# First expert: units in a meander, one sum of y over two FF tiles; relu(1 - e) by ScalarE in the second expert's regular groups; a new order

## The chip, the cores and the metric

One core of one Trainium2 chip runs the whole program. The metric is the device time of one execution in microseconds: the median of three runs of the kernel before is 793.62 us (793.28 to 793.9). TensorE is written PE, VectorE DVE, ScalarE ACT, GpSimd POOL, SyncE SP.

## The reference

Attention with hashed buckets, then two dense experts on the same 1536 tokens:

```
q_bucket, k_bucket = 6 sign bits of q @ proj, k @ proj          # 2 x 8 heads, 768 x 64
attn   = softmax(where(q_bucket == k_bucket, q @ k.T / 8, -1e9)) @ v
x      = attn, heads side by side                               # 1536 x 512
xn     = x / sqrt(mean(x * x) + 1e-6) * rms_g
g, val = xn @ w_gate, xn @ w_val                                # FF 1536
y      = (g * sigmoid(g) * val) @ w_out                         # the first expert
h      = y @ w_in                                               # FF 2048
out    = where(h > 0, h, exp(min(h, 0)) - 1) @ w2_out           # the second expert
```

The weights arrive as 64-bit floats and are turned into 32-bit words on the chip. Every product of both experts is made of three matmuls on pairs of fp32r tiles, a rounded part ("hi") and what the rounding left ("lo"): hi x hi, hi x lo, lo x hi.

## The kernel before, in words

**Attention** goes over 8 pairs of heads, 6 units of two query tiles each: scores (`ps_s`), their maximum by DVE, exp by ACT, transposes (`ps_p`), hi and lo parts by ACT and DVE or POOL, and the product with v (`ps_v`).

**The first expert** has 12 FF tiles of 128. Three of them form a regular group (`hidden`, group 0). The other nine are units of their own, n = 0 to 8: `pair(q, j, prio)` takes both batches at once for half of the columns, j = 0 or 1, and makes two 2 x 2 products out of seven (banks `ps_wA`, `ps_wC`, `ps_wE`, 6 matmuls of 384 columns for each product, L1520). It leaves two activated tiles h, o = 0 for column block j and o = 1 for block 2 + j, in the pool `ptp` of `PTS` = 4 tiles. `reduce1` then multiplies such a tile with w_out for each of the m = 0 to 3 output slices (L1160, bank `ps_y`) and DVE adds the bank to the running sum `ya` in SBUF (L1172). After the last unit `hi` and `lo` of `reduce1` split `ya` into the tiles `y` (L1177 by ACT, L1181 by DVE), which the second expert reads. The order of the units before is n = 0 to 8, and j = 0, 1 within each n; every unit's tiles are summed alone:

```
n, first, last = (groups[0][2], True, False) if g == 0 else (1, False, g == ("w", (0, NPW[0] - 1)))
```

**The second expert** has two regular groups of two FF tiles, each over four column blocks of 384 (`hidden`, L1067), and then six units of `pair`. In a regular group ACT makes e = exp(h) (L1095), `d2` on DVE makes min(e, 1) - 1 (L1104), `d3` adds max(h, 0) (L1110), then ACT and DVE split the result (L1116, L1120), and `reduce2` multiplies with w2_out (L1220). Beside the first of these groups `spread_t` combines the blocks of `ya` and splits the results for the second expert's units (L1260, L1267, L1271, on POOL, DVE and ACT), and the weights of the regular groups are converted by `c1` to `c5`, `hi` and `lo` of `weights` (L964 to L1016).

**The order of the work** is written out by hand: each piece of work is a task of the class `Plan`, and the table `ORDER` says in which order the tasks are issued. An engine works through its own tasks in that order; a task waits for what it reads and for a free buffer of its pool. The pools around the change: `ps1` (four PSUM banks, for `ps_wA`, `ps_wC`, `ps_wE`, `ps_h`), `ps2` (two double banks, for `ps_y` and `ps_o`), `ptp` (four h tiles), and `hlf` with `H3S` = 14 tiles of 3 KB, for loads and converted weights.

Of the kernel before, what the change touches and what calls it, by code (L numbers as in the profile page):

```python
# [9 lines left out]
F32R = mybir.dt.float32r  # L10
# [10 lines left out]
SLOTS, H3S, PTS = 22, 14, 4  # L21
# [209 lines left out]
]  # L231


# [1588 lines left out]
```

## Time and profile before

| what | us |
|---|---|
| median of 3 runs | 793.62 |
| the profiled execution, whole | 793.52 |
| its span | 791.7 |
| PE busy | 773.1 (98%) |
| DVE busy | 699.9 (88%) |
| ACT busy | 518.1 (65%) |
| POOL busy | 474.6 (60%) |

The span begins with attention (0 to some 230 us), then comes the first expert's regular group (to 300), its nine units (to some 530), the second expert's regular groups, and from 586 on the second expert's units. PE's busy time counts matmuls that overlap their neighbours and have stretched ends, so 98% doesn't mean that PE is at its peak: how many matmuls fit into a stretch tells more. The granted TensorE clock is full nearly throughout (0.999).

### The profile page before, as it was taken

Reading aid. Unit: us, or ns where it says so; the run is one execution under the profiler, and the core shown is the slowest. Engines: PE = TensorE matmul, PEld = TensorE weight load, DVE = VectorE, ACT = ScalarE, POOL = GpSimd, SP = SyncE. Lnnn points to the kernel's source line nnn. Section 1 sums busy time; section 2 is a strip of 40 time slices with the busy share of each in tenths; the row PEclk is TensorE's granted clock in tenths of the full one; section 3 lists DMA queues with packets and bytes.
Section 4 is the critical chain, followed back from the end, with each engine's and each line's share of the span. In section 5 each row is a group of like instructions: output and inputs, shape, how many; then the busy total and the mean of one; then the engine's idle time right before and its main releaser. Section 6 shows DMA issues by size and latency. Waiting matters only on the chain.

```text
span 791.7 us, 13077 instructions
## 1 busy us (share of the span) xinstructions
PE 773.1 (98%) x4618; PEld 726.1 (92%) x4618; DVE 699.9 (88%) x1147; ACT 518.1 (65%) x1078; POOL 474.6 (60%) x480
## 2 busy tenths in 40 slices
PE   8999999999999999999999999978999999999998
PEld 7999899998999999999999999967899889988987
DVE  7898999999985976889989899999888989888885
ACT  7999999989984636554444554556456666657553
POOL 7898899989886277555545554454534453633520
PEclk9999999999999999999999999999999999999999
DMA  5547563461000001222111312311021121131104
GB/s 197 190 134 233 193 176 94 142 180 31 27 28 1 27 1 54 81 81 70 65 52 54 107 55 80 115 45 51 4 80 54 54 81 54 54 97 63 54 2 158
DMA packets 33649, 65.74 MB, mean 83 GB/s; under 512 B 3504, under 2 KB 13104, under 8 KB 33584
## 3 DMA queue, kind: packets, MB, share of 16 engines
q1 hardware_dynamic: 33584, 64.91, 25.9%
q8 instruction: 36, 0.59, 0.3%
q14 instruction: 29, 0.24, 0.1%
HBM read 56.25 MB, written 3.15 MB: 75 GB/s over the span
## 4 chain that ended last, share of the span: by engine, by line
PE 77%; DVE 16%; ACT 3%; issue 2%; DMA 1%; POOL 0%; ACTq 0%; DVEq 0%; POOLq 0%
PE ps_o L1220 16%; PE ps_wA L1520 14%; PE ps_y L1160 10%; PE ps_h L1067 8%; PE ps_wC L1520 7%; PE ps_v L711 6%; PE ps_s L619 6%; PE ps_p L664 5%; PE ps_wE L1520 3%; DVE ya L1172 2%; DVE nm L626 2%; DVE pt L676 2%; DVE y L1181 1%; ACT p L636 1%; DVE h L1598 1%
## 5 line engine op out<-in xcount | busy, mean ns | idle before, releaser
L1458 POOL TENSOR_TENSOR W<-wf,W 128x256 fp32r<-128x256 f32 x105 | 86.9, 841 | 59.7 <-ACT W L1454 56.0
L1220 PE MATMUL ps_o<-whi,h 128*128 128x512 f32 (+1 forms) x388 | 119.6, 389 | 2.4 <-DVE h L1120 2.4
L1160 PE MATMUL ps_y<-h,whi 128*128 128x384 f32 x528 | 115.5, 338 | 4.3 <-DVE ya L1172 4.0
L1520 PE MATMUL ps_wA<-T,W 128*128 128x384 f32 x540 | 108.3, 335 | 0.0
L1160 PEld LDWEIGHTS ps_y<-h,whi 128*128 128x128 f32 x528 | 92.5, 188 | 9.0 <-DVE ya L1172 7.0
L1520 PEld LDWEIGHTS ps_wA<-T,W 128*128 128x128 f32 x540 | 95.3, 188 | 2.1 <-ACT wt L1538 0.3
L626 DVE TENSOR_REDUCE nm<-ps_s 128x1 f32<-128x768 f32 x96 | 91.0, 949 | 4.6 <-PE ps_s L619 3.6
L711 PE MATMUL ps_v<-pt,vv 128*128 128x256 f32 x576 | 94.4, 292 | 0.6 <-DVE pt L676 0.6
L636 ACT ACTIVATE p<-ps_s,nm 128x768 f32<-128x768 f32 x96 | 87.4, 911 | 5.6 <-DVE nm L626 4.1
L619 PE MATMUL ps_s<-tk,tq 128*128 128x384 f32 x384 | 87.2, 349 | 2.2 <-ACT p L636 1.7
L676 DVE TENSOR_TENSOR pt<-ps_p,pt 128x512 fp32r<-128x512 f32 x120 | 80.1, 683 | 8.0 <-ACT pt L672 6.7
L1172 DVE TENSOR_TENSOR ya<-ps_y,ya 128x384 f32<-128x384 f32 x144 | 76.6, 550 | 11.6 <-PE ps_y L1160 11.2
L1220 PEld LDWEIGHTS ps_o<-whi,h 128*128 128x128 f32 x388 | 72.0, 188 | 14.8 <-DVE h L1120 2.8
L664 PE MATMUL ps_p<-ident,p 128*128 128x128 f32 x576 | 82.4, 274 | 1.4 <-DVE pt L676 1.0
L711 PEld LDWEIGHTS ps_v<-pt,vv 128*128 128x128 f32 x576 | 79.6, 189 | 2.7 <-DVE pt L676 1.0
L1377 POOL TENSOR_SCALAR wf<-wf 128x512 f32<-128x512 f32 x51 | 38.1, 748 | 66.5 <-ACT wf L1374 63.5
L1444 POOL TENSOR_TENSOR wf<-wf 128x256 f32<-128x256 f32 x60 | 48.8, 813 | 47.5 <-DVE wf L1393 46.5
L1220 PE MATMUL ps_o<-wlo,h 128*128 128x512 f32 (+1 forms) x194 | 76.1, 392 | 0.0
L672 ACT CAST pt<-ps_p 128x512 fp32r<-128x512 f32 x120 | 68.9, 589 | 8.1 <-PE ps_p L664 5.0
L664 PEld LDWEIGHTS ps_p<-ident,p 128*128 128x128 f32 x576 | 66.6, 141 | 7.1 <-DVE pt L676 1.4
L1233 DVE TENSOR_TENSOR oa<-ps_o,oa 128x512 f32<-128x512 f32 (+1 forms) x85 | 57.1, 680 | 14.9 <-PE ps_o L1220 14.6
L619 PEld LDWEIGHTS ps_s<-tk,tq 128*128 128x128 f32 x384 | 63.1, 189 | 6.2 <-ACT p L636 4.6
(159 smaller groups left out, 1799.0 us busy)
## 6 DMA issues: line engine op xcount, KB each, us to landing
wraw<-in_moe_w_out_dram SPq DMA_DIRECT2D x25, 512.0 KB, 3.3
wraw<-in_moe_w_in_dram SPq DMA_DIRECT2D x16, 512.0 KB, 3.8
qk<-in_heads_dram SPq DMA_DIRECT2D x16, 384.0 KB, 5.1
qq<-in_heads_dram SPq DMA_DIRECT2D x14, 384.0 KB, 5.2
kk<-in_heads_dram SPq DMA_DIRECT2D x14, 384.0 KB, 4.9
wraw<-in_moe_w_gate_dram SPq DMA_DIRECT2D x18, 256.0 KB, 2.8
wraw<-in_moe_w_val_dram SPq DMA_DIRECT2D x18, 256.0 KB, 3.1
tq<-tq SPq DMA_DIRECT2D x21, 192.0 KB, 2.8
```

The lines of the kernel that those rows point to most:

```text
L619: nc.tensor.matmul(st[B_][:, hf, 0:HS], lhsT=tq[:, x, c * 128:(c + 1) * 128], rhs=tk[:, x, hf * HS:(hf + 1) * HS], start=(x == 0), stop=(x ...
L626: nc.vector.tensor_reduce(out=st["nm", u, cc], in_=st[B_][:, :, 0:HS], axis=AX.XY, op=ALU.max, negate=True,)
L636: nc.scalar.activation(out=halves(st["p", u][:, cc]), in_=st.pop(B_)[:, :, 0:HS], func=AF.Exp, bias=st["nm", u, cc], scale=1.0, accum_out= ...
L664: nc.tensor.transpose(out=st[B_][:, o:o + 128], in_=p[:, cc, (2 * n + kt) * 128:(2 * n + kt + 1) * 128], identity=ident,)
L672: nc.scalar.copy(out=st[T_][:, 0], in_=st[B_])
L676: nc.vector.tensor_tensor(out=pt[:, 1], in0=st.pop(B_), in1=f(pt[:, 0]), op=ALU.subtract)
L711: nc.tensor.matmul(st[B_][:, 0:256], lhsT=st["vv", j][:, a, 2 * n + kt, :], rhs=pt[:, x, kt * 256:(kt + 1) * 256], start=(n == seq[0] and ...
L1160: nc.tensor.matmul(s["ps"][:, 0:bw], lhsT=wo[wp][:, ft, m * 128:(m + 1) * 128], rhs=h[:, xp, 0:bw], start=(ft == 0 and i == 0), stop=(ft = ...
L1172: nc.vector.tensor_tensor(out=ya, in0=s["ps"][:, 0:bw], in1=ya, op=ALU.add)
L1220: nc.tensor.matmul(s["ps"], lhsT=h[:, xp, t * 128:(t + 1) * 128], rhs=(wo[wp][ft][:, 0] if reg2(g) else wo[wp][:, ft])[:, ds], start=(ft = ...
L1458: nc.gpsimd.tensor_tensor(out=t[:, 1], in0=blk(*src), in1=f(t[:, 0]), op=ALU.subtract)
L1520: nc.tensor.matmul(s[bk], lhsT=w[:, wp, k], rhs=x[:, xp, cs], start=start and k == 0 and i == 0, stop=k == 1 and i == 2, skip_group_check= ...
```

## The change

Five things change in the code, and the table `ORDER` with them.

1. The units of the first expert run in a meander: (0, j=1), then (0, 0) and (1, 0), then (1, 1) and (2, 1), then (2, 0) and (3, 0), and so on to (7, 1) and (8, 1), and (8, 0) alone. Two units with the same j that follow each other form a row, and `reduce1` takes their two FF tiles into one PSUM bank: six matmuls, and then one addition to `ya`. There are 10 rows, so 80 additions instead of 144; the matmuls stay 432.
2. The last tiles of blocks 1 and 3 come before those of 0 and 2, and the second expert's first group takes the blocks in the order 1, 3, 0, 2.
3. In the second expert's regular groups `a2` on ACT makes relu(1 - e), with a bias from SBUF, in place of `d2` on DVE, and `d3` subtracts it: 16 instructions go from DVE to ACT.
4. The two tiles `bitt` of attention move to the pool `tmp`, under the tag of the units' `wt` tiles, and `H3S` is 15 instead of 14.
5. The gates of the weights' loads follow the new sequence.

```diff
-SLOTS, H3S, PTS = 22, 14, 4
+SLOTS, H3S, PTS = 22, 15, 4
...
-    0, 3, 1, 6, 45, 46, 8, 9, 10, 11, 12, 13, 14, 15, 16, 42, 43, 7, 54, 44, 5, 28, 29, 17, 18, 19, 20, 51, 24, 25,
...
-    bitt = [const.tile([128, S // 2], F32R, name=f"bitt{i}") for i in range(2)]
+    bitt = [tmp.tile([128, S // 2], F32R, tag="wt", name=f"bitt{i}") for i in range(2)]
...
-        def d2():
-            nc.vector.tensor_scalar(
-                out=s["sg"], in0=s["sg"], scalar1=1.0, scalar2=1.0, op0=ALU.min, op1=ALU.subtract
-            )
+        def a2():
+            nc.scalar.activation(out=s["sg"], in_=s["sg"], func=AF.Relu, bias=ones[:, 0:1], scale=-1.0)
...
-                out=s["hf"], in0=s[0][:, 0:bw], scalar=0.0, in1=s["sg"], op0=ALU.max, op1=ALU.add
+                out=s["hf"], in0=s[0][:, 0:bw], scalar=0.0, in1=s["sg"], op0=ALU.max, op1=ALU.subtract
...
-            plan.add("DVE", 0.46, d2, [], [G_], prio)
+            plan.add("ACT", act(bw, 1), a2, [], [G_], prio)
...
-        n, first, last = (groups[0][2], True, False) if g == 0 else (1, False, g == ("w", (0, NPW[0] - 1)))
+        n, first, last = (groups[0][2], True, False) if g == 0 else (len(g), False, (0, NPW[0] - 1) in g)
...
-            wo = st["w", g]["wo"]
+            wo = st["w", g]["wo"] if g == 0 else st["w", ("w", g[ft])]["wo"]
...
+    rows = [[(0, 1)]]
+    for n in range(NPW[0]):
+        rows.append([(x, n % 2) for x in (n, n + 1) if x < NPW[0]])
+    seen = set()
+    for row in rows:
+        for n, j in row:
+            pair((0, n), j, pos)
...
+            pos += 2.0
+            for pg, pb in late:
+                for m in range(KD):
+                    reduce1(pg, pb, m, pos)
+            late = []
+            pos += 1.0
+        late = [(tuple((0, n) for n, _ in row), j), (tuple((0, n) for n, _ in row), 2 + j)]
+    for g in range(1, len(groups)):
...
+        for n, blk in enumerate((1, 3, 0, 2) if g == 1 else (0, 2, 1, 3)):
```

Where the order moves. PE in the middle of the first expert's units, before (`ps_w` are the seven products, `ps_y` the products with w_out; three matmuls are one sum):

```order
L1520 MATMUL ps_wE<-xn,W 128x384 x6
L1160 MATMUL ps_y<-h,whi 128x384 x6
L1520 MATMUL ps_wA<-T,W 128x384 x6
L1160 MATMUL ps_y<-h,whi 128x384 x6
L1520 MATMUL ps_wC<-xn,W 128x384 x6
L1160 MATMUL ps_y<-h,whi 128x384 x6
L1520 MATMUL ps_wA<-xn,W 128x384 x6
L1520 MATMUL ps_wA<-T,W 128x384 x6
L1160 MATMUL ps_y<-h,whi 128x384 x6
```

The same place on PE after the change, where six matmuls are one sum:

```order
L1511 MATMUL ps_wA<-T,W 128x384 x6
L1151 MATMUL ps_y<-h,whi 128x384 x12
L1511 MATMUL ps_wA<-T,W 128x384 x6
L1511 MATMUL ps_wA<-xn,W 128x384 x6
L1151 MATMUL ps_y<-h,whi 128x384 x24
L1511 MATMUL ps_wA<-T,W 128x384 x6
L1511 MATMUL ps_wE<-xn,W 128x384 x6
L1511 MATMUL ps_wC<-T,W 128x384 x6
L1151 MATMUL ps_y<-h,whi 128x384 x12
```

Eight sums of one unit each stood between the products in 24 matmuls; now eight sums of two units each stand there in 48, in fewer and longer runs.

DVE where the first expert meets the second, before (`ya<-ps_y` is a sum, `y_` the split of the finished sum, `sg<-sg` is `d2`, `hf<-ps_h` is `d3`, `h<-hf` a split of an activated tile):

```order
L1172 TENSOR_TENSOR ya<-ps_y,ya 128x384 x2
L1104 TENSOR_SCALAR sg<-sg 128x384
L1172 TENSOR_TENSOR ya<-ps_y,ya 128x384
L1181 TENSOR_TENSOR y_6540<-ya,y_6540 128x384
L1181 TENSOR_TENSOR y_6667<-ya,y_6667 128x384
L1172 TENSOR_TENSOR ya<-ps_y,ya 128x384
L1110 SCALAR_TENSOR_TENSOR hf<-ps_h,sg 128x384
L1172 TENSOR_TENSOR ya<-ps_y,ya 128x384
L1181 TENSOR_TENSOR y_6551<-ya,y_6551 128x384
L1181 TENSOR_TENSOR y_6634<-ya,y_6634 128x384
L1181 TENSOR_TENSOR y_6646<-ya,y_6646 128x384 x2
L1172 TENSOR_TENSOR ya<-ps_y,ya 128x384 x2
```

DVE at that place after the change:

```order
L1172 TENSOR_TENSOR y_6516<-ya,y_6516 128x384
L1172 TENSOR_TENSOR y_6542<-ya,y_6542 128x384
L1172 TENSOR_TENSOR y_6505<-ya,y_6505 128x384
L1172 TENSOR_TENSOR y_6424<-ya,y_6424 128x384
L1172 TENSOR_TENSOR y_6460<-ya,y_6460 128x384
L1163 TENSOR_TENSOR ya<-ps_y,ya 128x384
L1172 TENSOR_TENSOR y_6488<-ya,y_6488 128x384
L1163 TENSOR_TENSOR ya<-ps_y,ya 128x384
L1101 SCALAR_TENSOR_TENSOR hf<-ps_h,sg 128x384
L1163 TENSOR_TENSOR ya<-ps_y,ya 128x384
L1172 TENSOR_TENSOR y_6464<-ya,y_6464 128x384
L1172 TENSOR_TENSOR y_6516<-ya,y_6516 128x384
```

The sums of blocks 0 and 2 are still between the splits, `d2` is gone, and the splits of blocks 1 and 3 stand ahead of all of `d3`.

PE at the same joint, before (`ps_h<-y` are the second expert's first matmuls, 12 for each FF tile and block):

```order
L1520 MATMUL ps_wC<-xn,W 128x384 x6
L1160 MATMUL ps_y<-h,whi 128x384 x6
L1520 MATMUL ps_wA<-T,W 128x384 x6
L1160 MATMUL ps_y<-h,whi 128x384 x6
L1067 MATMUL ps_h<-y_6540,whi 128x384 x2
L1067 MATMUL ps_h<-y_6540,wlo 128x384
L1067 MATMUL ps_h<-y_6551,whi 128x384 x2
L1067 MATMUL ps_h<-y_6551,wlo 128x384
```

PE there after the change:

```order
L1511 MATMUL ps_wE<-xn,W 128x384 x6
L1511 MATMUL ps_wA<-T,W 128x384 x6
L1151 MATMUL ps_y<-h,whi 128x384 x18
L1511 MATMUL ps_wA<-T,W 128x384 x6
L1151 MATMUL ps_y<-h,whi 128x384 x33
L1060 MATMUL ps_h<-y_6424,whi 128x384 x2
L1060 MATMUL ps_h<-y_6424,wlo 128x384
L1060 MATMUL ps_h<-y_6460,whi 128x384 x2
L1060 MATMUL ps_h<-y_6460,wlo 128x384
```

Seven groups of matmuls for y, four of six and three of three, stand between the last product of the first expert and the first matmul of the second, where there were two of three.

## Rows read from the trace of the kernel before

**Rows 1.** Windows: microseconds, then busy time (instructions) by engine, clock, DMA share, GB/s.

```profile
0.00:230.00 230.00, 224.03 (x1649) 208.08 (x1650) 215.76 (x332) 211.25 (x429) 202.23 (x193) 1.00 0.44 138
300.00:467.00 167.00, 167.00 (x961) 166.08 (x960) 145.18 (x262) 84.64 (x189) 90.36 (x107) 1.00 0.22 70
467.00:561.00 94.00, 84.78 (x455) 78.35 (x453) 91.99 (x149) 47.04 (x97) 48.81 (x44) 1.00 0.21 68
600.00:776.00 176.00, 176.00 (x881) 158.60 (x880) 151.82 (x254) 113.50 (x241) 76.03 (x87) 1.00 0.18 56
```

**Rows 2.** Chain that ended last, 465 to 570 us: start us, us, what.

```profile
466.20 1.05 PE ps_wA L1520 x6
467.28 0.56 DVE hf L1541
...
526.98 3.76 DVE y L1181 x4
...
531.67 1.77 DVE sg L1104
533.45 2.08 DVE y L1181
```

**Rows 3.** Windows of line L1220 alone, 467 to 561 us.

```profile
467.00:561.00 94.00, 9.04 (x36) 6.65 (x36) 1.00 0.21 68
```

**Rows 4.** Chain of the whole span, after 561 us.

```profile
563.50 1.39 PE ps_o L1220 x6
```

**Rows 5.** Waits of PE, 467 to 561 us: us in total, times, longest us.

```profile
PE ps_y L1160 <- DVE ya L1172: 4.0, 8, 1.4
PE ps_o L1220 <- DVE h L1120: 2.4, 1, 2.4
PE ps_h L1067 <- DVE y L1181: 1.8, 1, 1.8
```

**Rows 6.** Lines of DVE, 467 to 561 us: busy us, mean ns, idle before.

```profile
L1172 DVE TENSOR_TENSOR ya<-ps_y,ya 128x384 f32<-128x384 f32 x48 | 25.2, 546 | 0.6 <-PE ps_y L1160 0.4
L1181 DVE TENSOR_TENSOR y<-ya,y 128x384 fp32r<-128x384 f32 x16 | 12.1, 789 | 1.0 <-ACT y L1177 1.0
L1598 DVE TENSOR_TENSOR h<-hf,h 128x384 fp32r<-128x384 f32 x11 | 7.2, 665 | 0.0
L1104 DVE TENSOR_SCALAR sg<-sg 128x384 f32<-128x384 f32 x6 | 6.9, 1150 | 0.0
L987 DVE SCALAR_TENSOR_TENSOR wf<-wraw,wf 128x512 int32<-128x512 int32 x6 | 6.0, 999 | 0.0
L1120 DVE TENSOR_TENSOR h<-hf,h 128x384 fp32r<-128x384 f32 x5 | 4.3, 879 | 0.2 <-ACT h L1116 0.2
L973 DVE TENSOR_SCALAR wf<-wf 128x512 int32<-128x512 int32 x6 | 4.1, 678 | 0.0
L980 DVE SCALAR_TENSOR_TENSOR wf<-wraw,wf 128x512 int32<-128x512 int32 x6 | 4.0, 678 | 0.0
```

**Rows 7.** Timelines of DVE and of POOL at 541 us, and of DVE at 551.

```profile
541.83 2.01 DVE L1104 TENSOR_SCALAR sg<-sg 128x384 f32<-128x384 f32 x1
...
541.42 2.20 POOL L1260 TENSOR_TENSOR ya<-ya 128x768 f32<-128x768 f32 x1
...
551.21 0.35 DVE L1104 TENSOR_SCALAR sg<-sg 128x384 f32<-128x384 f32 x1
```

**Rows 8.** Lines of ACT over the whole span: relu(1 - e) in the units.

```profile
L1557 ACT ACTIVATE sg<-sg,ones 128x384 f32<-128x384 f32 x48 | 29.5, 617 | 1.2
```

**Rows 9.** Timeline of PE and of DVE: a group's matmuls, and its sum.

```profile
479.64 1.20 PE L1160 MATMUL ps_y<-h,whi 128*128 128x384 f32 x6
...
482.54 0.54 DVE L1172 TENSOR_TENSOR ya<-ps_y,ya 128x384 f32<-128x384 f32 x1
```

**Rows 10.** Waits of ACT, 300 to 467 us.

```profile
ACT h L1594 <- DVE hf L1588: 13.8, 10, 2.4
```

**Rows 11.** Chain around 77 us: start us, us, what.

```profile
77.33 5.01 DMA kk<-in_heads_dram
```

More of the change, by code (lines that the diff above doesn't have):

```diff
@@ L1138, in h1 @@
     def h1(g, blk, ft):
-        return ("h", g, blk, ft) if g == 0 else ("wh", g[1], blk % 2, blk // 2)
+        return ("h", g, blk, ft) if g == 0 else ("wh", g[ft], blk % 2, blk // 2)
     def reduce1(g, blk, m, prio):
-        n, first, last = (groups[0][2], True, False) if g == 0 else (1, False, g == ("w", (0, NPW[0] - 1)))
+        n, first, last = (groups[0][2], True, False) if g == 0 else (len(g), False, (0, NPW[0] - 1) in g)
         bw = width(g)
         cs = slice(blk * bw, (blk + 1) * bw)
-        B_ = ("bank2", "y", g, blk, m)
+        B_ = ("bank2", "y", g if g == 0 else ("w", g[-1]), blk, m)
         A_ = ("slot", "ya", m)
@@ L1160, in pe @@
                 nc.tensor.matmul(
-                    s["ps"][:, 0:bw], lhsT=wo[wp][:, ft, m * 128:(m + 1) * 128], rhs=h[:, xp, 0:bw],
+                    s["ps"][:, 0:bw], lhsT=wo[wp][:, ft if g == 0 else 0, m * 128:(m + 1) * 128], rhs=h[:, xp, 0:bw],
                     start=(ft == 0 and i == 0), stop=(ft == n - 1 and i == 2),
@@ L1183, in reduce1 @@
         hk = [(("pt", *h1(g, blk, ft)), p) for ft in range(n) for p in range(2)]
-        wk = wkeys(g, 2) if g == 0 else [(("slot", "who", g), p) for p in range(2)]
+        wk = wkeys(g, 2) if g == 0 else [(("slot", "who", ("w", q)), p) for q in g for p in range(2)]
         plan.add("PE", 3 * n * mm(bw), lambda: [pe(ft) for ft in range(n)], hk + wk, [B_], prio)
@@ L1728 @@
     late = [(0, prev)]
-    for li in range(2):
-        reduce_, nr = (reduce1, KD) if li == 0 else (reduce2, 3)
-        if li:
-            for g in range(1, len(groups)):
-                todo = wtasks(g + 1) if g + 1 < len(groups) else []
-                for n, blk in enumerate((0, 2, 1, 3)):
-                    for pg, pb in late:
-                        for m in range(KD if not reg2(pg) else 3):
-                            (reduce1 if not reg2(pg) else reduce2)(pg, pb, m, pos)
-                    if g == 1 and n == 0:
-                        spread_t()
-                    for ft in range(groups[g][2]):
-                        hidden(g, blk, ft, pos)
-                        hid += 1
-                        pos += 1.0
-                    late = [(g, blk)]
-                    if n == 0:
-                        for x in todo:
-                            weights(*x, pos + 0.5, [("hgo", hid - 2)])
-                        if not todo:
-                            pair_weights((1, 0), pos + 4, [("hgo", hid - 2)] if g > 1 else [("wgo", (0, NPW[0] - 1), 0)])
-        for n in range(NPW[li]):
-            for j in range(2):
-                pair((li, n), j, pos)
-                if j == 0:
-                    if n + 1 < NPW[li]:
-                        pair_weights((li, n + 1), pos + 1, [("wgo", (li, n), 0)])
-                    elif li == 0:
-                        for todo in wtasks(1):
-                            weights(*todo, pos + 0.5, [("wgo", (li, n - 1), 0)])
-                pos += 2.0
-                for pg, pb in late:
-                    for m in range(KD if li == 0 else 3):
-                        reduce_(pg, pb, m, pos)
-                pos += 1.0
-                late = [(("w", (li, n)), j), (("w", (li, n)), 2 + j)]
@@ new lines @@
+    rows = [[(0, 1)]]
[5 more added lines that the diff above has]
+            pair((0, n), j, pos)
+            if n not in seen:
+                seen.add(n)
+                if n + 1 < NPW[0]:
+                    pair_weights((0, n + 1), pos + 1, [("wgo", (0, n), j)])
+                else:
+                    for x in wtasks(1):
+                        weights(*x, pos + 0.5, [("wgo", (0, n - 1), 1 - j)])
+            pos += 2.0
[5 more added lines that the diff above has]
+        late = [(tuple((0, n) for n, _ in row), j), (tuple((0, n) for n, _ in row), 2 + j)]
@@ new lines @@
+    for g in range(1, len(groups)):
+        todo = wtasks(g + 1) if g + 1 < len(groups) else []
+        for n, blk in enumerate((1, 3, 0, 2) if g == 1 else (0, 2, 1, 3)):
+            for pg, pb in late:
+                for m in range(KD if not reg2(pg) else 3):
+                    (reduce1 if not reg2(pg) else reduce2)(pg, pb, m, pos)
+            if g == 1 and n == 0:
+                spread_t()
+            for ft in range(groups[g][2]):
+                hidden(g, blk, ft, pos)
+                hid += 1
+                pos += 1.0
+            late = [(g, blk)]
+            if n == 0:
+                for x in todo:
+                    weights(*x, pos + 0.5, [("hgo", hid - 2)])
+                if not todo:
+                    pair_weights((1, 0), pos + 4, [("hgo", hid - 2)])
@@ L1765 @@
+    for n in range(NPW[1]):
+        for j in range(2):
+            pair((1, n), j, pos)
+            if j == 0 and n + 1 < NPW[1]:
+                pair_weights((1, n + 1), pos + 1, [("wgo", (1, n), 0)])
+            pos += 2.0
+            for pg, pb in late:
+                for m in range(3):
+                    reduce2(pg, pb, m, pos)
+            pos += 1.0
+            late = [(("w", (1, n)), j), (("w", (1, n)), 2 + j)]
     for pg, pb in late:
```

380 rows, old and new, of the table ORDER are left out of this document.

## The prediction

> **What bounds the kernel now.** I read first the table of busy time by stage, then the chain of waits, then the waits and the costliest lines of the one stage where PE loses time, last two timelines in it.
>
> In the table by stage [rows 1] the reader is to look at how many matmuls fit into a stretch, not at PE's busy time. From 300 to 467 us, in the first expert's units, PE runs 961 matmuls in 167 us without a gap: 0.1738 us each, all of 384 columns. From 600 to 776 PE is as dense. In neither can a faster DVE gain anything; both are bound by PE, and the change leaves PE's matmuls as they are, 432 for y among them. Attention (0 to 230) is a tie: PE 224, DVE 216, ACT 211, POOL 202 us of 230.
>
> The stretch from 467 to 561, where the first expert ends and the second begins, is the other thing: DVE is busy 92.0 of 94 us. The chain of waits shows the same [rows 2]: up to 466.2 it is PE alone, from 467.3 on it is DVE, sums `ya`, splits `y`, the step `sg`; only after 561 PE has it again. What PE needs there: 36 of the 455 matmuls are the second expert's of 512 columns [rows 3], at 1.39/6 = 0.232 us [rows 4], so 8.3 us; the other 419 at 0.1738 give 72.8; together 81.1 us. PE loses 94.0 - 81.1 = 12.9 us there. PE's waits name who ended them [rows 5]: DVE's sums, DVE's split of `h`, DVE's split of `y` (they add up to less than 12.9, since a stretched matmul hides part of a gap). These 12.9 us are what the change can win outside attention.
>
> **The change part by part.**
>
> *Two FF tiles in one sum.* 64 of 144 sums go, 0.546 us each [rows 6]: 35 us of DVE. Most of them lie where PE bounds, beside its matmuls, and win nothing by themselves. Counted in the order over the same 81.1 us of PE's work ahead of 561, 48 sums become 29: 19 fewer, at 25.2/48 = 0.525 us of busy time each (neighbours overlap a little) 10.0 us.
>
> *relu(1 - e) by ACT.* Six `d2` lie in the stretch, 6.9 us, 1.150 on average [rows 6]. Alone such an instruction takes 0.35; those of 2 us stand beside a POOL instruction of the same length [rows 7]. So its going is worth between 6 x 0.35 = 2.1 us, if the wait for POOL passes to the next instruction of DVE, and 6.9, if it goes too. On ACT it costs 0.617 [rows 8], 3.7 us on top of 47.0 of 94 [rows 1]: hidden, ACT is half idle. Were it not, the chain exp, relu, maximum, splits would be 0.617 - 0.35 = 0.3 us longer for each tile, and four banks of `ps_h` let PE go on meanwhile.
>
> The rows show that `d2` is held beside POOL, and so are the splits: 0.789 on average for `y`, 0.546 for a sum of the same size that reads PSUM [rows 6]. The Trainium skill, SBUF — State Buffer, section "Who interferes with whom", says why this speaks against the edit: VectorE and GpSimd share one pair of SBUF ports as a lock for a whole instruction, and an instruction of VectorE with two SBUF inputs takes part in it as much as a two-port `tensor_scalar`. By that rule the split behind a missing `d2` takes over its wait, and the edit is worth 2.1 us, not 6.9. The trace agrees in that the sums, with one input in PSUM, stay at 0.546.
>
> *What that leaves.* Other DVE work moves in and out of the stretch by pieces (conversions and `d3` in, steps of the combination out) and about cancels. DVE's need falls from 92.0 to between 92.0 - 10.0 - 6.9 = 75.1 and 92.0 - 10.0 - 2.1 = 79.9 us, PE's stays 81.1. On average DVE no longer bounds, but its work comes in bursts, and I go by two legs of the new order.
>
> Leg A is the last 10.4 us of PE with products (ten groups of six matmuls, up to the last product of unit 8). DVE has there 5 joins of products and 6 sums and 3 gate products (0.546 each, the same shape: 7.6), 9 steps of weight conversion (3 x (0.678 + 0.678 + 0.999) = 7.1) and 2 splits of `h` (0.665 each, 1.3): 16.0 us, 5.6 too many. Leg B goes from there to the first product with w2_out: 4 groups of six and 8 of three for y, and six FF tiles of twelve: 120 matmuls, 20.9 us. DVE has 12 sums, 1 gate product, 3 `d3` (16 x 0.546 = 8.7) and 15 splits of `y`, 2 of the first expert's tiles, 2 of the second's: unhindered 19 x 0.546 = 10.4, at the means of rows 6 15 x 0.789 + 2 x 0.665 + 2 x 0.879 = 14.9. Together 19.1 to 23.6, -1.8 to +2.7 against PE. Both legs: 3.8 to 8.3 us too many.
>
> Not all of that stops PE. Before, PE went on without a gap while a sum started 2.2 us behind its matmuls: three of the six that start at 479.64 end by 480.3, and the sum starts at 482.54 [rows 9]. Less 2.2, PE loses 1.6 to 6.1 us. I take 5.0, in the upper half, because the splits' waits for POOL remain and the conversions for the second group follow closely. So the stage's loss goes from 12.9 to 5.0, and 7.9 us are won. The bounds: 12.9 won if all gaps close, 3 if the old bursts stay apart from the missing sums.
>
> *Four h tiles in a row of units.* A row fills all four buffers. The cast of the next unit's tile waits on ACT until the four sums of the first block are through, 24 matmuls, 4.2 us; behind it in ACT's queue stand the copies that free PSUM banks. Before, this cast waited 13.8 us in ten places [rows 10] with no gap of PE in the stretch [rows 1], and PE now has seven products of another unit, 7.3 us, to do at that point. I take 0; the bound is a rival below.
>
> *The 15th tile, `bitt`, the rest of the order.* In attention the same tasks stand a few places earlier or later, and no row prices this. PE is idle 6.0 us of 230 by busy time [rows 1], so I bound it by 3 either way, and by the 5.0 us for which a late load of `kk` stands in the chain once [rows 11] on the side of a gain, since a 15th tile lets loads start sooner. I take 0, the middle: what binds there is four engines at 88 to 97%, and their work is the same.
>
> **The sum**, against the profiled execution's own 793.52 us (span 791.7 and 1.8 around it): 793.5 - 7.9 = 785.6. The median of the runs shown is 0.1 above that execution, so 785.7.
>
> **The rivals.**
>
> 1. The stall stays, under other names. All 16 splits of `y`, all conversions and all the combination's steps still stand around the joint, and POOL still holds some of them. Then the 10.0 us of sums thin out DVE where PE bounds anyway, and only the 3 us or so remain that the legs can't take back: 790.5. For it: the splits are 12.1 us of the stretch and stay. Against it: blocks 1 and 3 are now finished a unit earlier, so that their splits lie beside seven products.
>
> 2. All gaps close, and the 15th tile wins 2 us in attention: 793.6 - 12.9 - 2 = 778.7. For it: 75.1 us of DVE against 81.1 of PE. Against it: leg A.
>
> 3. The new order of attention costs what the joint wins, or the joint wins little and attention loses: within 0.2% of before, 792 to 795. For it: attention is a third of the time and has no slack; against it: the work is the same, and PE's order there moves by a place or two.
>
> 4. Slower: rows hold the four h tiles. At each of the nine changes of row ACT's cast waits for a free tile, the copies behind it wait, a PSUM bank is late, and PE stands. This decides from 7.9/9 = 0.9 us for each change of row; at 1.5 us it costs 13.5 and the time is 793.6 - 7.9 + 13.5 = 799.2. For it: all four buffers are taken at once, which they were not before. Against it: PE has 7.3 us of products for 4.2 us of waiting.
>
> **How the numbers follow.** The forecast, 3.5 to 12 us won, has 0.66; rival 1 0.12, rival 2 0.09, rival 3 0.06, rival 4 0.07. About 0.2% (1.6 us) is what a measurement of this kernel can tell from no change. Faster by more: the forecast and rivals 1 and 2, 0.87; within it rival 3, 0.06; slower rival 4, 0.07. The range reaches from 779.0 (nearly all gaps closed, part of rival 2) to 790.5 (rival 1); what lies outside is rivals 3 and 4 and halves of 1 and 2, about 0.2.
>
> **What would show it.** Right: some 80 sums instead of 144 at 0.55 us; in the first expert's units still 0.174 us for each matmul; in the stage before the second expert's first regular tiles a loss of PE near 5 us, and DVE below 95% busy there; the chain on PE for most of the joint; 64 instead of 48 relu on ACT at 0.62; the splits of `y` no faster than 0.79. Wrong: PE gaps behind ACT's cast at changes of row (rival 4); attention ending more than 3 us away from where it ended; a loss at the joint of 9 us or more (rival 1) or below 1 (rival 2).

## The result, and the profile after

The changed kernel takes 784.95 us (median of 4 runs, 783.64 to 785.33), the kernel before beside it 793.76 (793.28 to 794.01): ratio 0.9887, 95% interval 0.987 to 0.9904. 785.7 was predicted. The profiled execution took 783.64 us, span 781.9, so 9.9 less than the one of before. It is the shortest of the four: by the medians 8.8 us are won.

Busy time by stage after the change, to be read against [rows 1]; the columns are the same.

```profile
0.00:230.00 230.00, 225.09 (x1658) 209.06 (x1659) 215.90 (x334) 212.95 (x430) 203.55 (x195) 1.00 0.44 138
300.00:467.00 167.00, 167.00 (x965) 166.94 (x964) 130.53 (x222) 85.83 (x193) 90.82 (x110) 1.00 0.23 73
467.00:561.00 94.00, 90.86 (x493) 85.58 (x492) 80.89 (x129) 57.02 (x115) 46.60 (x42) 1.00 0.20 62
600.00:776.00 176.00, 176.00 (x874) 157.86 (x873) 148.11 (x253) 110.35 (x234) 69.28 (x83) 1.00 0.20 66
```

The line of the matmuls of 512 columns alone, in the same stretch as [rows 3].

```profile
467.00:561.00 94.00, 11.81 (x50) 9.44 (x51) 1.00 0.20 62
```

Again the matmuls are counted. 493 fit into 467 to 561 us instead of 455. 50 of them have 512 columns: 50 x 0.232 + 443 x 0.1738 = 88.6 us of need, so PE loses 5.4 of 94 us where it lost 12.9. That is 7.5 of the 9.9 us. In attention 9 matmuls more fit into 230 us, at 230/1658 = 0.139 us each 1.3 us. From 300 to 467 there are 965 instead of 961, at most 0.7 us, while DVE went from 145.2 to 130.5 us: PE bounds there, and fewer sums won next to nothing. The rest of the 9.9 us, 1.1 with those 0.7, is spread, and is about as much as the profiled execution is shorter than the median.

DVE's lines in the stretch, to be read against [rows 6].

```profile
L1163 DVE TENSOR_TENSOR ya<-ps_y,ya 128x384 f32<-128x384 f32 x28 | 15.2, 549 | 2.7 <-PE ps_y L1151 2.7
L1172 DVE TENSOR_TENSOR y<-ya,y 128x384 fp32r<-128x384 f32 x16 | 12.5, 809 | 0.2
L966 DVE TENSOR_SCALAR wf<-wf 128x512 int32<-128x512 int32 x8 | 7.7, 972 | 0.0
L1111 DVE TENSOR_TENSOR h<-hf,h 128x384 fp32r<-128x384 f32 x8 | 7.5, 941 | 4.5 <-ACT h L1107 4.5
```

28 sums instead of 48, at the same 0.55 us. The splits of y are no faster, 0.81 us, nor are the other instructions here that read and write SBUF. Sums now wait 2.7 us for PE, and PE waits 0.9 us for sums where it waited 4.0. PE's waits, against [rows 5]:

```profile
PE ps_o L1211 <- ACT oa L1220: 1.3, 1, 1.3
PE ps_y L1151 <- DVE ya L1163: 0.9, 3, 0.5
PE ps_h L1060 <- DVE hf L1101: 0.7, 1, 0.7
```

relu(1 - e) on ACT over the whole span, in the units and in the regular groups (lines of ACT, against [rows 8]); then ACT's waits from 300 to 467 us that answer to [rows 10]:

```profile
L1548 ACT ACTIVATE sg<-sg,ones 128x384 f32<-128x384 f32 x48 | 29.2, 616 | 1.0
L1097 ACT ACTIVATE sg<-sg,ones 128x384 f32<-128x384 f32 x16 | 9.9, 618 | 0.4
```

```profile
ACT h L1585 <- PE ps_y L1151: 8.0, 2, 4.3
ACT h L1585 <- DVE hf L1579: 6.6, 6, 1.9
```

The cast of a fifth h tile does wait for PE's sums, up to 4.3 us where 4.2 were reckoned, but no wait of PE between 300 and 467 us follows from it.

What still stands at the joint: POOL's steps and DVE's splits side by side (start, us).

```profile
525.12 2.68 DVE L1172 TENSOR_TENSOR y<-ya,y 128x384 fp32r<-128x384 f32 x2
529.32 2.74 DVE L1172 TENSOR_TENSOR y<-ya,y 128x384 fp32r<-128x384 f32 x2
534.80 2.08 DVE L966 TENSOR_SCALAR wf<-wf 128x512 int32<-128x512 int32 x1
...
525.35 2.04 POOL L1251 TENSOR_TENSOR ya<-ya 128x768 f32<-128x768 f32 x1 [0.42 <-DVE ya L1163]
529.48 2.17 POOL L1251 TENSOR_TENSOR ya<-ya 128x768 f32<-128x768 f32 x1
534.44 2.15 POOL L1251 TENSOR_TENSOR ya<-ya 128x768 f32<-128x768 f32 x1
```

### The profile page after: what moved, and what is told of

Same layout as the page of the kernel before. It is cut to its first block, busy times and chain, and to the rows that moved or that the text cites. A ratio compares the mean times of both kernels' runs of the same rounds, so it can differ in the third digit from the quotient of the medians.

```text
span 781.9 us, 12995 instructions
## 1 busy us (share of the span) xinstructions
PE 770.5 (99%) x4618; PEld 726.0 (93%) x4618; DVE 663.8 (85%) x1067; ACT 527.5 (67%) x1094; POOL 470.8 (60%) x480
## 4 chain that ended last, share of the span: by engine, by line
PE 89%; DVE 7%; ACT 2%; issue 1%; DMA 1%; SPq 0%; DVEq 0%; ACTq 0%
PE ps_o L1211 17%; PE ps_wA L1511 16%; PE ps_y L1151 12%; PE ps_h L1060 9%; PE ps_wC L1511 8%; PE ps_s L612 7%; PE ps_v L704 7%; PE ps_p L657 7%; PE ps_wE L1511 4%; DVE nm L619 1%; DVE y L1172 1%; DVE pt L669 1%; PE ps_x L762 1%; PE ps_b L520 1%; ACT p L629 1%
## 5 line engine op out<-in xcount | busy, mean ns | idle before, releaser
L1151 PE MATMUL ps_y<-h,whi 128*128 128x384 f32 x528 | 107.6, 336 | 1.1 <-DVE ya L1163 0.9
L704 PE MATMUL ps_v<-pt,vv 128*128 128x256 f32 x576 | 92.8, 292 | 0.0
L657 PE MATMUL ps_p<-ident,p 128*128 128x128 f32 x576 | 84.2, 274 | 1.0 <-DVE pt L669 0.7
L1368 POOL TENSOR_SCALAR wf<-wf 128x512 f32<-128x512 f32 x51 | 36.5, 719 | 71.5 <-ACT wf L1365 62.0
L1163 DVE TENSOR_TENSOR ya<-ps_y,ya 128x384 f32<-128x384 f32 x80 | 43.2, 551 | 15.5 <-PE ps_y L1151 15.0
```

What stands on the lines that cost most here:

```text
L657: nc.tensor.transpose(out=st[B_][:, o:o + 128], in_=p[:, cc, (2 * n + kt) * 128:(2 * n + kt + 1) * 128], identity=ident,)
L704: nc.tensor.matmul(st[B_][:, 0:256], lhsT=st["vv", j][:, a, 2 * n + kt, :], rhs=pt[:, x, kt * 256:(kt + 1) * 256], start=(n == seq[0] and ...
L1151: nc.tensor.matmul(s["ps"][:, 0:bw], lhsT=wo[wp][:, ft if g == 0 else 0, m * 128:(m + 1) * 128], rhs=h[:, xp, 0:bw], start=(ft == 0 and i ...
```

## The experiments

Ratios are to the kernel before, run beside each; one thousandth is 0.8 us. The changed kernel once more, beside some of them:

> The changed kernel unchanged, as the measure for the runs beside it: 784 to 785 us, 0.987 to 0.990 of before.

784.69 us, ratio 0.9896 (0.9882 to 0.991). Where a run is called slower or faster than the changed kernel, it is measured from this ratio. In the other kernels the lines stand a few off (L1243 or L1252 for L1251).

**The sums taken apart.**

```diff
-                s["ps"] = bank2("ps_y")[:, 0]
+                s["ps"] = bank2("ps_y")
...
-            nc.vector.tensor_tensor(out=ya, in0=s["ps"][:, 0:bw], in1=ya, op=ALU.add)
+            for x in range(n):
+                nc.vector.tensor_tensor(out=ya, in0=s["ps"][:, x, 0:bw], in1=ya, op=ALU.add)
```

> The changed kernel with its sums undone: the two FF tiles of a row are multiplied at the same places of the order, but each into its own half of the double bank, and each is added to ya by itself. 64 more additions (80 to 144), matmuls, order and banks as in the changed kernel. Around the joint (467 to 561 us) 28 sums become 48 (those of the last unit alone stay single): 20 x 0.549 = 11.0 us more on DVE, which is busy 80.9 of 94 there. Theory (the fewer sums are what thinned DVE out at the joint): most of the gain of the joint goes, 4 to 8 us slower than the changed kernel, 789 to 793 us, and PE waits for DVE's sums again. Rival (the meander and the new order, blocks 1 and 3 finished a unit earlier, are the gain, the sums lie beside matmuls anyway): 784.5 to 786.5.

795.6 us, ratio 1.0031 (1.0019 to 1.0043): 10.7 us slower than the changed kernel, slower than before. By stage:

```profile
300.00:467.00 167.00, 164.81 (x933) 160.89 (x932) 144.25 (x254) 82.94 (x187) 85.97 (x104) 1.00 0.22 70
467.00:561.00 94.00, 87.23 (x469) 80.94 (x468) 85.00 (x149) 51.72 (x106) 46.92 (x46) 1.00 0.21 68
```

469 matmuls, 36 of 512 columns, are 83.6 us: 10.4 us lost between 467 and 561 us, 5.0 more. And in the units 32 matmuls fewer fit, 5.6 us, with DVE busy 144 of 167 us as before the change. But a kernel that is late by 467 us has other work in a window of fixed times. So here are windows that begin and end with the same work: from the first matmul of the second expert to the first product of its units, of the kernel before, the changed one and this one; then from the first product of the first expert's units to the first matmul of the second expert, of the last two.

```profile
517.82:586.24 68.42, 60.00 (x302) 53.01 (x301) 63.52 (x95) 38.00 (x75) 31.36 (x23) 1.00 0.10 31
518.72:579.96 61.24, 59.09 (x304) 53.81 (x304) 54.12 (x74) 44.61 (x85) 32.58 (x26) 1.00 0.15 46
530.71:591.94 61.23, 59.08 (x304) 53.83 (x304) 54.15 (x74) 44.55 (x85) 32.59 (x26) 1.00 0.14 46
...
295.98:518.72 222.74, 221.75 (x1270) 219.71 (x1270) 177.84 (x306) 114.69 (x255) 116.23 (x136) 1.00 0.25 79
296.44:530.71 234.27, 226.77 (x1270) 218.97 (x1270) 206.14 (x370) 115.11 (x255) 114.85 (x136) 1.00 0.24 75
```

The joint's gain lies in the first window, 68.42 to 61.24 us, and the single sums give none of it back: DVE does the same 74 instructions there, and the sums left in it, those of the last unit, are single in both. All 11.5 us are lost ahead of the second expert's first matmul, in the units and at the groups for y behind the last product. PE waits for sums again, as the theory said, but the place is another and the time above its range. So this run does not show that the fewer sums made the joint's gain. It shows that the new order can't do without them: with single sums it loses ahead of the joint more than it wins there, and the order before, where every unit is summed alone, did not. That its products for y come in longer runs, and that a double bank is free only after two sums, may be why; no run shows it. Neither side had expected the units.

**`d2` back on DVE, and `a2` alone in the kernel before.** The first edit, and the second is its reverse in the other kernel:

```diff
-            nc.scalar.activation(out=s["sg"], in_=s["sg"], func=AF.Relu, bias=ones[:, 0:1], scale=-1.0)
+            nc.vector.tensor_scalar(
+                out=s["sg"], in0=s["sg"], scalar1=1.0, scalar2=1.0, op0=ALU.min, op1=ALU.subtract
+            )
```

> The changed kernel with min(e, 1) - 1 back on DVE in the second expert's regular groups, in the same places of the order: 16 instructions go from ACT back to DVE. Theory (the wait beside POOL passes on to the next instruction of DVE, so that such a step is worth what it takes alone, 0.35 us; eight of them around the joint are 2.8 us, part of which DVE's slack takes): 0 to 2 us slower than the changed kernel, 785 to 787. Rival (each is worth its whole 1.15 us of before): 16 x 1.15 = 18 us more of DVE, 9 at the joint, 4 to 8 us slower, 789 to 793. Second rival (ACT was loaded by it, and the copies that free the PSUM banks wait less): 0.5 to 1.5 us faster, 783.5 to 784.5.

> The kernel before with relu(1 - e) on ACT instead of d2 on DVE in the second expert's regular groups, its order kept: that edit alone. Theory (a step that goes takes what it costs alone and some of its wait along, as in the changed kernel, where undoing it cost 3 us): 789.5 to 792 us. Rival (in the old order DVE has so much queued at the joint that the next instruction takes over every wait beside POOL): 792.5 to 794. Second rival (the six steps of 1.15 us go whole): 786.5 to 788.

787.94 us, ratio 0.993 (0.9918 to 0.9942), 2.7 us slower than the changed kernel, above the theory's 2; and 791.82 us, ratio 0.9979 (0.9969 to 0.9988), 1.7 us faster than before, inside it. DVE's splits of y at the joint, with `d2` back in the changed kernel and with `a2` in the one before:

```profile
L1174 DVE TENSOR_TENSOR y<-ya,y 128x384 fp32r<-128x384 f32 x16 | 10.3, 675 | 0.1
```

```profile
L1179 DVE TENSOR_TENSOR y<-ya,y 128x384 fp32r<-128x384 f32 x16 | 11.9, 779 | 1.5 <-ACT y L1175 1.5
```

With `d2` on DVE the splits take 0.675 us, without it 0.809: the wait beside POOL passes to whichever instruction stands there. In the kernel before it did not pass to the splits of y (0.779 us with `a2`, 0.789 before), but the first step of the weights went from 0.678 us [rows 6] to 0.979:

```profile
L973 DVE TENSOR_SCALAR wf<-wf 128x512 int32<-128x512 int32 x7 | 6.9, 979 | 0.0
```

There sixteen `d2` are gone, six of them in the stretch, and 1.7 us are won (1.0 to 2.5 by the interval), near the six's 2.1 alone and far from 6.9. ACT's sixteen instructions may not be free: PE's one wait for ACT's copy `oa`, 1.3 us in the changed kernel, is 0.2 with `d2` back on DVE. From the second expert's first matmul to the first product of its units the kernel with `d2` back takes 2.3 us more than the changed one:

```profile
519.33:582.82 63.49, 59.73 (x304) 53.70 (x304) 58.42 (x88) 37.03 (x71) 33.62 (x26) 1.00 0.15 48
```

So `d2` carries 2.3 of the 7.2 us that the change wins there. The sums carry none of it, nor does the 15th tile: with 14 tiles the same stretch takes 61.24 us again (522.46 to 583.70). The other 4.9 are left to the order, that is the meander and the blocks 1 and 3 first. This is by elimination; no run has the order alone, or these two apart.

**14 tiles in the changed kernel, 15 in the kernel before.**

```diff
-SLOTS, H3S, PTS = 22, 15, 4
+SLOTS, H3S, PTS = 22, 14, 4
...
-    bitt = [tmp.tile([128, S // 2], F32R, tag="wt", name=f"bitt{i}") for i in range(2)]
+    bitt = [const.tile([128, S // 2], F32R, name=f"bitt{i}") for i in range(2)]
```

> The changed kernel with 14 instead of 15 tiles h3 and the two tiles bitt back in their own place, the order kept. Theory (the 15th tile lets loads and conversions start sooner, and that is what attention gained): 1 to 2 us slower than the changed kernel, 786 to 787, lost before 240 us. Rival (the order of attention gained it, no buffer is short): 784.5 to 785.5. Second rival (the order is made for 15 tiles, and with 14 loads in the experts come late too): 788 or more, with DMA in the chain after 300 us.

> The kernel before with 15 instead of 14 tiles h3 and the two tiles bitt in the units' pool, its own order kept. Theory (the 15th tile is worth as much without the new order as 14 tiles cost the changed kernel, that is 2.8 us in attention and 2.5 near 600 us): 788 to 791 us, won in attention above all. Rival (the old order was made for 14 tiles and asks for no fifteenth at any time that counts; the tile pays only with the order made for it): within 1 us of before.

With 14 tiles 789.55 us, ratio 0.9956 (0.9943 to 0.9969): 4.8 us slower. With 15 in the kernel before 794.39 us, ratio 1.0004 (0.9996 to 1.0013): nothing. The changed kernel with 14 tiles: its window over attention, and ACT's timeline near 595 us (start, us, idle before):

```profile
0.00:230.00 230.00, 222.49 (x1635) 205.72 (x1636) 213.96 (x329) 209.69 (x424) 199.93 (x191) 1.00 0.44 138
```

```profile
594.75 0.66 ACT L1365 ACTIVATE wf<-wraw 128x512 f32<-128x512 f32 x1 [7.62 <-issue]
```

1635 matmuls instead of 1658 are 3.2 us. A late load of `kk` stands in the chain there. None of nine traces of the new order with 15 tiles has one; of the old order's three, one with 14 tiles [rows 11] and the one with 15 have it, at 77 us. In the chain of the changed kernel with 14 tiles, and of the kernel before with 15:

```profile
124.99 5.04 DMA kk<-in_heads_dram
...
77.34 5.83 DMA kk<-in_heads_dram
```

At 594.75 ACT stood 7.62 us at the first step of a weight's conversion, with nothing that the profile names to wait for (a tile of `h3` is what that step needs, and one tile is what was taken away); a cast and an exp stood behind it, and PE waited 1.4 us. So the first run's theory has the place (attention) and too small a price; its second rival has the time, 788 or more, and the loss in the experts, but no load stands in the chain after 300 us as it said. In the second run the rival is right: the tile is worth nothing by itself, and 4.8 us to an order that counts on it.

**POOL's steps later.** POOL's order at the joint:

```diff
-L1251 TENSOR_TENSOR ya<-ya 128x768 x2
-L1262 TENSOR_TENSOR T<-ya,T 128x768
-L1251 TENSOR_TENSOR ya<-ya 128x768
 L960 TENSOR_SCALAR wf<-wf 128x512 x2
-L1251 TENSOR_TENSOR ya<-ya 128x768
 L960 TENSOR_SCALAR wf<-wf 128x512 x2
+L1251 TENSOR_TENSOR ya<-ya 128x768 x2
 L1009 TENSOR_TENSOR wlo<-wf,whi 128x512 x2
+L1251 TENSOR_TENSOR ya<-ya 128x768 x2
+L1262 TENSOR_TENSOR T<-ya,T 128x768
```

> The changed kernel with POOL's four steps of the combination of y and its split of T moved behind POOL's weight steps for the second group, so that they start near 538 instead of 523 us, behind the last split of y; the casts that follow them and one step of DVE move along. The work is the same. Theory (POOL's steps of 2 us hold DVE's splits of y, and with them the sums that PE waits for): the splits of y fall from 0.81 us on average to below 0.65, PE's loss between 525 and 545 falls, 1 to 3 us faster than the changed kernel, 782 to 784. Rival (the splits are as late because DVE has too much to do anyway): 784.5 to 785.5. Second rival (POOL is now late for the low parts of the second group's weights or for T): the loss turns up between 545 and 590 us, 786 to 789.

789.09 us, ratio 0.9945 (0.9933 to 0.9957): 3.9 us slower. The splits of y did fall to the time they take alone:

```profile
L1164 DVE TENSOR_TENSOR y<-ya,y 128x384 fp32r<-128x384 f32 x16 | 8.9, 585 | 0.2
```

But POOL now stood beside the conversions and the splits of h, and PE waited 4.6 us for the `d3` behind them. The timelines of DVE and of POOL from 545 to 556 us, and then the windows over PE's gap and behind it (the columns of [rows 1], the granted clock behind POOL's):

```profile
547.59 4.06 DVE L958 TENSOR_SCALAR wf<-wf 128x512 int32<-128x512 int32 x2
551.57 2.16 DVE L1103 TENSOR_TENSOR h<-hf,h 128x384 fp32r<-128x384 f32 x1
553.65 2.28 DVE L965 SCALAR_TENSOR_TENSOR wf<-wraw,wf 128x512 int32<-128x512 int32 x1
...
545.40 3.96 POOL L1243 TENSOR_TENSOR ya<-ya 128x768 f32<-128x768 f32 x2
549.33 6.05 POOL L1254 TENSOR_TENSOR T<-ya,T 128x768 fp32r<-128x768 f32 x3
```

```profile
551.00:556.00 5.00, 0.88 (x6) 0.56 (x4) 5.00 (x4) 0.74 (x2) 4.38 (x3) 1.00 0.00 0
556.10:559.50 3.40, 3.05 (x10) 3.05 (x11) 3.19 (x5) 2.98 (x6) 1.07 (x1) 0.50 0.02 5
```

Four instructions of DVE in a row take as long as POOL's beside them, though they take 0.41 to 0.68 alone. The theory of the hold is right and its forecast wrong: here the hold was not lost by moving it, it was only given to other instructions. The second rival has the place and, at 789.09 for 786 to 789, all but the time, by another way than it said.

**POOL's eight instructions on DVE, or cut in two.**

```diff
-                (nc.gpsimd if i in TPOOL else nc.vector).tensor_tensor(
+                nc.vector.tensor_tensor(
...
-                lambda: sub(nc.gpsimd if gp else nc.vector, to, x, y, prio), r, ks(*to), prio,
+                lambda: sub(nc.vector, to, x, y, prio), r, ks(*to), prio,
```

> The changed kernel with the eight instructions of POOL in the combination of y (four steps, four splits of T) on DVE, at the same places of the order. POOL's take 2.0 to 2.2 us each, a step on DVE 0.95: DVE gets 8 x 0.95 = 7.6 us more. Theory (DVE's SBUF instructions are held beside POOL's): the holds go, that is of the changed kernel's means between 467 and 561 us 16 x (0.81 - 0.55) for the splits of y, 8 x (0.94 - 0.55) for those of h, 8 x (0.97 - 0.41) for the first weight step, together 11.8 us; DVE is 4 us better off, the time 782 to 785. Rival (the holds have another cause, or DVE's own queue is what counts): DVE is 7.6 us worse off where it is 86% busy, PE loses 3 to 6 us more, 788 to 791.

782.92 us, ratio 0.9868 (0.9855 to 0.9882): 2.2 us faster than the changed kernel by the ratios, 1.8 by the medians. The two intervals touch, but all four executions (782.4 to 783.47 us) lie below all five of the changed kernel beside them (784.35 to 786.3).

```profile
L1172 DVE TENSOR_TENSOR y<-ya,y 128x384 fp32r<-128x384 f32 x16 | 8.9, 586 | 0.1
L1251 DVE TENSOR_TENSOR ya<-ya 128x768 f32<-128x768 f32 x8 | 8.0, 1002 | 0.0
L1111 DVE TENSOR_TENSOR h<-hf,h 128x384 fp32r<-128x384 f32 x8 | 4.6, 569 | 4.9 <-ACT h L1107 4.9
L966 DVE TENSOR_SCALAR wf<-wf 128x512 int32<-128x512 int32 x8 | 4.4, 560 | 0.0
```

Against the changed kernel's lines above, the splits of y, the splits of h and the first weight step lose 3.6, 2.9 and 3.3 us. DVE does eight instructions more and is busy 80.64 us instead of 80.89.

```diff
-            eng.tensor_tensor(out=o, in0=a, in1=c, op=ALU.subtract)
+            for q in ((slice(0, HS), slice(HS, S)) if eng is nc.gpsimd else (slice(0, S),)):
+                eng.tensor_tensor(out=o[:, q], in0=a[:, q], in1=c[:, q], op=ALU.subtract)
```

> The changed kernel with the same eight instructions of POOL cut into two of 384 columns each, on POOL as before. Theory (an instruction of DVE waits for the end of the one POOL instruction beside it, so a hold is as long as that): holds fall from up to 2 us to some 1 us, 1 to 2 us faster than the changed kernel, 783 to 784. Rival (POOL keeps what DVE needs through a row of its own instructions): 784.5 to 786, and DVE's instructions of 2 us stay.

783.56 us, ratio 0.9875 (0.9862 to 0.9889): 1.1 us faster by the medians, 1.7 by the ratios, about the least that can be told from none; its four executions (782.91 to 783.84) lie below the same five. The longest of DVE's instructions between 525 and 560 us went from 2.2 to 1.76 us (that one a step of 768 columns), those of 384 and 512 columns to 1.5. In the timelines of DVE and of POOL (start, us):

```profile
531.11 1.37 DVE L1111 TENSOR_TENSOR h<-hf,h 128x384 fp32r<-128x384 f32 x1
...
530.73 2.62 POOL L1252 TENSOR_TENSOR ya<-ya 128x384 f32<-128x384 f32 x2
```

DVE's split ends at 531.11 + 1.37 = 532.48, before POOL's pair does at 530.73 + 2.62 = 533.35: DVE gets in between two of POOL's instructions.

**The conversions later, and what was left of the gaps.** DVE's order at the joint, in the first of three kernels (the three steps stand there twice, for two tiles); in the second POOL's eight instructions are on DVE besides; of the third the main moves are shown, against the second:

```diff
-L966 TENSOR_SCALAR wf<-wf 128x512
-L973 SCALAR_TENSOR_TENSOR wf<-wraw,wf 128x512
-L980 SCALAR_TENSOR_TENSOR wf<-wraw,wf 128x512
...
 L1163 TENSOR_TENSOR ya<-ps_y,ya 128x384
+L966 TENSOR_SCALAR wf<-wf 128x512
+L973 SCALAR_TENSOR_TENSOR wf<-wraw,wf 128x512
+L980 SCALAR_TENSOR_TENSOR wf<-wraw,wf 128x512
```

```diff
 L1164 TENSOR_TENSOR y_6491<-ya,y_6491 128x384
+L1243 TENSOR_TENSOR ya<-ya 128x768
 L1103 TENSOR_TENSOR h<-hf,h 128x384
...
-L1243 TENSOR_TENSOR ya<-ya 128x768 x3
+L1254 TENSOR_TENSOR T<-ya,T 128x768
+L1243 TENSOR_TENSOR ya<-ya 128x768 x2
```

> The changed kernel with the six DVE steps of converting w2_out for the second expert's first group moved some 18 us down the order, from between 503 and 512 us to between 524 and 530, their casts on ACT and low parts on POOL with them. They take 3.9 us. Theory (between 498 and 519 us DVE simply has more work than PE, so that 2.8 us of PE are lost, whatever POOL does): the loss of PE before 519 us falls below 1 us. Behind it DVE's splits now share DVE with the conversions and POOL's steps, and 1 to 4 us are lost there anew: 784 to 787. Rival (the gaps before 519 come from the sums' place in the order, not from how much there is): the loss before 519 stays above 2 us, 785 to 788.

> The same move of the conversions, with the eight instructions of POOL in the combination of y on DVE, and of these the four steps and the first split moved behind 543 us, where DVE was idle for 2.8 us. Theory (DVE's work before 519 us and the holds beside POOL are the two causes of what PE still loses at the joint, 6.1 us): both losses fall below 1 us, 779.5 to 781.5 us, faster than the changed kernel and than the one with the steps on DVE in their old places (782.9). Rival (the conversions keep their tiles 18 us longer, and the second group's weights come late): a loss between 545 and 570 us, 783 to 786.

> The last kernel (conversions later, combination of y on DVE) with its three new losses taken up: the sum at 524 us, which waited 1.3 us behind the moved conversions, is put ahead of them; of the four steps of the combination one each goes into DVE's idle places near 532, 535 and 538 us and one behind 542; and the first split of T moves from 560 to 542 us, since the tile of the output that ACT's copy filled at 561 waited for it. Theory (the rest of the joint's loss is these places, not an amount of work): PE's loss from 490 to 570 us falls to 1 to 2.5 us, 779.5 to 782 us. Rival (DVE has too much work between 498 and 560 in sum, so that whatever is taken out of one gap opens another): 783 to 786.

788.62 us, ratio 0.9942 (0.993 to 0.9955); 785.7, ratio 0.9903 (0.989 to 0.9917); 784.39, ratio 0.9878 (0.9861 to 0.9895). So the first is 3.6 us slower than the changed kernel, the second 0.6 slower and the third 1.4 faster by the ratios (0.3 by the medians); the last two can't be told from it. None beats 782.92, and all three miss their theory's time. The windows ahead of and behind 519 us, of the changed kernel and then of the last of the three:

```profile
467.00:519.00 52.00, 51.01 (x286) 49.03 (x285) 44.15 (x80) 25.75 (x57) 24.05 (x27) 1.00 0.32 102
519.00:561.00 42.00, 39.85 (x209) 36.55 (x208) 36.73 (x50) 31.26 (x59) 22.55 (x15) 1.00 0.05 13
```

```profile
467.00:519.00 52.00, 51.72 (x293) 50.40 (x293) 41.73 (x77) 26.03 (x58) 21.43 (x25) 1.00 0.30 102
519.00:561.00 42.00, 38.57 (x200) 35.03 (x200) 40.22 (x61) 30.97 (x58) 10.48 (x9) 1.00 0.05 13
```

Ahead of 519 the loss fell, if not below 1 us: 286 matmuls need 49.7 of 52 us, 293 need 50.9, so 2.3 became 1.1. Behind it, 209 with 50 of 512 columns need 39.2 of 42, 200 with 49 need 37.6: 2.8 became 4.4. DVE is busy 40.22 of 42 us there. Each gap closed opened another. Of the rivals only the third kernel's was right. The first kernel's has neither the place (291 matmuls ahead of 519 leave 1.4 us, not above 2) nor the time; the second's has the time and the place, 545 to 570 us, but not the cause, which was no late weight. In the second kernel one of these was of a kind that nobody had named: PE waited 2.2 us for ACT's copy into `oa`, and the copy began right behind the split of T that had been moved to 560 us. In the third kernel this split stands ahead, on the reading that `oa` needs the place that the split sets free; the wait at 561 went, and others came.

## Why the prediction was right

**PE's bound, and the joint as the place.** Held: 7.5 of 9.9 us came from there, 7.9 were predicted, and the loss left is 5.4 instead of 5.0. DVE is busy 81 of 94 us there, 86%, as the prediction's "below 95%" had it.

**The sums.** The term of 10.0 us of DVE was right as an amount: 20 sums fewer, at 0.55 us, between 467 and 561 us. As the cause of the joint's gain it isn't shown, and by the windows on the same work it isn't: the 7.2 us won behind the second expert's first matmul stay won with single sums. "Win nothing by themselves" elsewhere is true against the order before, but with single sums the new order loses 11.5 us ahead of that matmul. So sums and order are one edit, and the prediction priced the sums alone. That its 7.9 came so near is in part luck.

**`d2`.** I left the worth of six between 2.1 and 6.9 us, with the Trainium skill's rule for the low end. It is the low end: 1.7 in the old order, 2.7 in the new one, for all sixteen each time. The wait did pass on, in the old order to the first weight step and not to the splits of y that the working named. The rule of the Trainium skill, SBUF — State Buffer, section "Who interferes with whom", that VectorE and GpSimd exclude each other for whole instructions, is borne out by three runs: holds of 2.0 to 2.3 us beside POOL's instructions of 2.0, of at most 1.5 us for 384 and 512 columns when these are cut in two, and splits of y at 0.586 us, against 0.809, when the eight are gone.

**The two legs.** The sum came out, its parts did not, and that too is luck. Leg A was 5.6 - 2.2 = 3.4 us; PE has no wait in it. Some 2 us are lost right behind it, at the groups for y up to 518.7 us, where PE's three waits for sums stand. In the rest of leg B, up to the first product with w2_out at 534.2, PE lost 0.4 us, though its upper half was taken for POOL's sake. So the legs lost some 2.5 us, in the lower half of 1.6 to 6.1. Some 2.5 more came behind them, at the next products with w2_out and the next tiles of h, where PE waits for ACT's copy `oa` (1.3) and for `d3` (0.7). That POOL's holds made these late fits their going down with POOL's instructions on DVE (0.7 and none). The legs ended too early: the burst went on behind them.

**ACT, and four h tiles.** As said for the tiles: PE has no gap at the changes of row, and rival 4 is out. Not quite for ACT: it is busy only 57 of 94 us, but PE's longest wait of the stretch, 1.3 us, is now for ACT's copy `oa`, and with `d2` back on DVE, which moves other instructions too, it is 0.2. "Hidden" was too much.

**The 15th tile.** This step failed. I took 0, because "what binds there is four engines at 88 to 97%, and their work is the same". Without the tile the same order loses 4.8 us, with the tile alone the old order won nothing, and attention won 1.3 us by the two traces. Less of that can be counted on: nine traces have the same instructions of attention and 15 tiles, and the first product of the units starts in them between 295.98 us (the changed kernel's) and 296.89. In two traces of the old order with 14 tiles it starts at 300.82 and 301.48, with 24 more matmuls ahead of it, 4.2 us. That is 0.65 us on average. By the letter a sign of being wrong came: attention's last product with v starts 3.1 us later than before (248.44 against 245.31). But 27 more matmuls stand ahead of it. The buffers decide whether the new order runs, and a price of 0 for an edit that belongs to an order is no price. The bound of 3 us on attention held. What the missing tile costs showed at a late load of `kk` (5.04 us in the chain), and near 595 us as 7.62 us of ACT's idle time that nothing ends in the profile.

**The sum.** 785.6 against 783.64 in the profiled executions: 0.4 us less won at the joint than said, 1.3 in attention and 1.1 elsewhere that were not reckoned with. By the medians it is 785.7 against 784.95, 0.75 us: the profiled execution is 1.3 us shorter than the median, so over half of what came unreckoned is that one execution. Rivals 1 and 3 are out; of rival 2 the joint's part did not come, and of attention's 2 us at most 1.3.

## What to carry to other kernels

Price the removal of an instruction on VectorE that stands beside GpSimd at no more than it takes alone: here the next one took over the wait. Compare two kernels over the same work, not only over the same times: a window of fixed times put a loss at the joint that lay ahead of it. Eight GpSimd instructions moved to VectorE won time although VectorE was the busy engine; count the holds they cause, not only the work they take. A buffer, or a joint sum, and the order written for it are one edit: what undoing one of them costs is not what it would win alone.

## What the hardware did that was not expected

With POOL's steps later, PE stood 4.6 us, and its granted clock was then 0.50 from 556.1 to 559.5 us, the lower of its two levels (1.2 GHz). The nine matmuls of 384 columns that start in this stretch took 3.05 us, where at 0.174 us each they take 1.56. So this gap cost some 1.5 us more than its length; gaps below 2 us in the changed kernel left the clock at 1.00. The length of a gap alone does not tell it: in the kernel before with 15 tiles the clock fell behind a wait of 1.8 us, and in the kernel before it stayed full behind one of 2.4 [rows 5]. The window of that fall:

```profile
536.80:540.20 3.40, 3.40 (x13) 3.40 (x12) 2.75 (x6) 3.40 (x7) 0.49 (x1) 0.50 0.03 7
```

Of 49 executions of the kernel before beside the experiments, 36 have a mean granted clock of 0.998 (median 793.7 us) and six of 1.000 (792.8); the nine of the changed kernel have 0.999 or 1.000. So up to 0.9 us of the gain by the medians may be clock, which nobody had reckoned with; the two profiled executions have no such fall before their last 2 us.

A step of 768 columns on POOL takes 2.0 us and on DVE 0.95, and in the traces of before and after no instruction of DVE with all its operands in SBUF begins and ends within one of these steps at the joint. At this joint POOL was no help but a lock.
